# Scores of the first four head pairs from undivided float32 operands, 1e-9 as one more column of each score row, and a new set of due offsets, in a thresholded-attention and gated-mix kernel

## The chip, the cores and the metric

The kernel runs on one core of one Trainium2 chip. A time is device microseconds of that core for one execution. The profiled execution has its own time and a span, from its first instruction to its last; what lies around the span is launch and end.

## The reference, cut to what matters

There are 8 batches with 8 heads of 576 rows and 64 dimensions. The weights come in float64, everything else in float32.

```
scores = (q @ k.T) / sqrt(64)                     # per batch and head, 576 x 576
keep   = scores >= max(scores, -1) - tau
attn   = where(keep, exp(scores - max), 0)
attn   = attn / (sum(attn, -1) + 1e-9)
x      = attn @ v                                 # heads side by side: 576 x 512 per batch
gate   = sigmoid(sum_k conv_w[k] * x shifted by 4 - k rows)
out    = (gate * (x @ w_val)) @ w_out
```

## The kernel before, in words

**Pairs and tiles.** Two heads form a pair, and 4 pairs a batch: 32 pairs, each a `Job`. A pair's scores are cut into 9 tiles of 128 rows by 576 keys: for each of four blocks of 128 query rows one tile per head (h = 0 and h = 1), and one tile (h = None, the corner) that holds the first 64 query rows of both heads. There are 288 tiles, counted by k. A tile runs through TensorE (`multiply`, L732), the row maximum on VectorE (`largest`, L736), the threshold (`lowest`, L742, VectorE), the exponential on ScalarE (`weigh`, L746), and masking with the row sum on VectorE (`keep`, L753). Two tiles then form a group (a corner tile is one by itself): GpSimd adds 1e-9 to the sums (L770), VectorE takes reciprocals (`inv`, L772), GpSimd, ScalarE or VectorE divide (L779 to L783), TensorE transposes the result (L836), and ScalarE copies it out of PSUM (L847). When a pair's tiles are through, `attend` multiplies with v on TensorE (L876 and L883, later L914 and L922).

**Products in parts.** To keep float32 accuracy at TensorE's fast rate, q and k are split into a high and a low float32r part (L441 to L461: ScalarE makes the high part, GpSimd the low part), and the parts are copied by 16 DMAs per pair into operands in which the 128 contraction rows are 64 of one kind over 64 of another: `Q` holds the high and the low part of q one above the other, `KH` the high part of k twice, `KL` the low part twice. A head's tile is then four matmuls with 128 contraction rows (two halves of 288 keys, KH and KL each); a corner tile is six from `bdq`. The first pair has no time for that: `load_at_once` loads its operands already doubled and splits them itself (L579 to L615, corners L596 and L600), and its corner tile takes ten matmuls (L719).

**The mix.** After attention a pair's x goes through the five-tap convolution on VectorE (L993, four taps a pair; the first on GpSimd, L988). After the fourth pair of a batch come its 192 products with w_val and w_out (L1052). The weights are put together from their float64 words on VectorE, ScalarE and GpSimd (`from_f64`, L321 to L339, eight blocks).

**Order.** Every engine's order is fixed when the program is built. Each operation has a planned cost, a due time (its tile's number plus an offset from the table `EARLY` for tiles below 78 and from `AT` after them), and rooms (buffers) that it takes and gives; `carry_out` picks, again and again, the operation that can start first and is due first. An operation may have several engines to choose from. Queues run in that order; a late instruction holds back all that stands behind it on its engine. Where the plan sees TensorE idle for over 1 us before 115 us, it puts in products of the identity matrix that nothing reads (L181, `keep_busy`), and it starts the program with 11 of them; each is two instructions in the trace. Score rooms in PSUM: three until tile `THIRD_UNTIL`, then two, and the third one's banks become the accumulators of the products.

## Time and profile before

| what | value |
|---|---|
| median of 3 runs | 730.72 us (730.11 to 732.25) |
| the profiled execution | 731.91 us, of which span 730.1 us, so 1.8 us around it |
| TensorE busy | 710.7 us (97%) |
| VectorE busy | 659.6 us (90%) |
| ScalarE busy | 593.0 us (81%) |
| GpSimd busy | 470.7 us (64%) |

PE is TensorE, PEld its weight loads, DVE VectorE, ACT ScalarE, POOL GpSimd, SP the queue that issues most DMAs. A matmul's duration in the trace holds its way through the array, which overlaps with the next one; what a matmul really takes from the engine is the distance between two starts.

### The profile page before, as it was taken

To read this page: it belongs to the slowest core of one execution; us is meant where nothing else is said; L and a number is where in the kernel's file an instruction comes from. 1 tells how busy PE (TensorE), PEld (TensorE's weight loads), DVE (VectorE), ACT (ScalarE), POOL (GpSimd) and SP (SyncE) were. 2 spreads that over 40 slices of the span, in tenths; PEclk is the share of its full clock that TensorE was granted. 3 is DMA by queue.
4 is the path that set the end of the run, shared out by engine and by line. 5 is a ranking of instruction groups with operands and counts; after the bars stand their busy time and mean duration, and the time that the engine had idled before them with its cause. 6 is when DMAs were issued, how large, how long until landed. Compare 5 with 4: busy or idle time off the path is not lost.

```text
span 730.1 us, 16335 instructions
## 1 busy us (share of the span) xinstructions
PE 710.7 (97%) x5338; PEld 618.5 (85%) x5338; DVE 659.6 (90%) x1618; ACT 593.0 (81%) x1167; POOL 470.7 (64%) x690
## 2 busy tenths in 40 slices
PE   9889889999999999999999999999999999999998
PEld 9666667988888998888889888888988888898988
DVE  5989989999999988999999999999999999899842
ACT  5999988888878988877889887887978887898730
POOL 2787757887677747686566765667566865655231
PEclk9999989999999999999999999999999999999999
DMA  6777656527564665456665555556655446540001
GB/s 210 196 198 193 152 140 175 119 58 200 151 165 115 166 170 141 103 135 156 152 164 129 145 139 152 146 123 153 177 136 132 118 138 170 140 101 19 34 33 66
DMA packets 60884, 100.55 MB, mean 138 GB/s; under 512 B 18688, under 2 KB 20096, under 8 KB 60800
## 3 DMA queue, kind: packets, MB, share of 16 engines
q1 hardware_dynamic: 60512, 98.96, 52.7%
q8 instruction: 43, 0.70, 0.4%
q10 hardware_dynamic: 288, 0.56, 0.2%
q14 instruction: 41, 0.34, 0.1%
HBM read 35.18 MB, written 9.44 MB: 61 GB/s over the span
## 4 chain that ended last, share of the span: by engine, by line
PE 86%; DVE 7%; ACT 3%; issue 1%; DMA 1%; POOL 1%; SPq 0%; POOLq 0%; ACTq 0%; DVEq 0%
PE acc L1052 26%; PE s L732 20%; PE tp L836 17%; PE acc L922 9%; PE tp L922 6%; DVE pp L753 2%; PE tp L181 2%; PE acc L914 2%; DVE nm L736 2%; PE tp L914 2%; ACT e L746 1%; ACT T L847 1%; DMA KH<-kh 1%; PE tp L883 1%; DVE pre L993 1%
## 5 line engine op out<-in xcount | busy, mean ns | idle before, releaser
L736 DVE TENSOR_REDUCE nm<-s 128x1 f32<-128x576 f32 x276 | 204.8, 753 | 25.5 <-PE s L732 22.8
L746 ACT ACTIVATE e<-s,nm 128x576 f32<-128x576 f32 x276 | 204.4, 754 | 16.1 <-DVE nm L736 13.8
L753 DVE SCALAR_TENSOR_TENSOR pp<-s,th,e 128x576 f32<-128x576 f32 x244 | 196.9, 813 | 8.7 <-ACT e L746 4.4
L847 ACT COPY T<-tp 128x384 f32<-128x384 f32 x384 | 175.1, 493 | 17.8 <-PE tp L836 16.5
L836 PE MATMUL tp<-ident,pp 128*128 128x128 f32 x1152 | 176.8, 274 | 7.5 <-ACT T L847 5.1
L732 PE MATMUL s<-KH,Q 128*128 128x288 f32 x488 | 148.7, 321 | 4.2 <-DVE pp L753 3.5
L836 PEld LDWEIGHTS tp<-ident,pp 128*128 128x128 f32 x1152 | 137.1, 140 | 15.5 <-ACT T L847 7.9
L732 PE MATMUL s<-KL,Q 128*128 128x288 f32 x488 | 136.5, 296 | 0.0
L783 POOL TENSOR_SCALAR pp<-pp,sums 128x576 f32<-128x576 f32 x132 | 106.4, 811 | 27.7 <-DVE sums L772 12.0
L993 DVE SCALAR_TENSOR_TENSOR pre<-xT,cw,pre 128x576 f32<-128x576 f32 x128 | 119.8, 938 | 0.7
L732 PEld LDWEIGHTS s<-KH,Q 128*128 128x128 f32 x488 | 92.5, 190 | 18.7 <-issue 8.2
L779 ACT ACTIVATE pp<-pp,sums 128x576 f32<-128x576 f32 x102 | 79.4, 791 | 21.8 <-DVE sums L772 21.4
L770 POOL TENSOR_SCALAR sums<-sums 128x2 f32<-128x2 f32 (+1 forms) x160 | 45.0, 281 | 75.6 <-DVE pp L753 61.7
L732 PEld LDWEIGHTS s<-KL,Q 128*128 128x128 f32 x488 | 92.7, 190 | 0.0
L1052 PE MATMUL acc<-gh,woh 128*128 128x256 f32 (+1 forms) x256 | 78.8, 308 | 0.0
L1052 PE MATMUL acc<-xh,wvh 128*128 128x256 f32 (+1 forms) x256 | 78.5, 307 | 0.3 <-DVE pp L753 0.2
L1052 PE MATMUL acc<-gh,wol 128*128 128x256 f32 (+1 forms) x256 | 78.5, 307 | 0.0
L1052 PE MATMUL acc<-xh,wvl 128*128 128x256 f32 (+1 forms) x256 | 78.4, 306 | 0.0
L1052 PE MATMUL acc<-gl,woh 128*128 128x256 f32 (+1 forms) x256 | 78.1, 305 | 0.0
L1052 PE MATMUL acc<-xl,wvh 128*128 128x256 f32 (+1 forms) x256 | 77.8, 304 | 0.0
L447 POOL TENSOR_TENSOR kl<-k_r,kh 128x320 fp32r<-128x320 f32 x62 | 57.4, 933 | 25.4 <-ACT kh L441 15.9
L461 POOL TENSOR_TENSOR ql<-q_r,qh 128x320 fp32r<-128x320 f32 (+1 forms) x62 | 59.2, 971 | 21.8 <-ACT qh L455 20.6
(116 smaller groups left out, 1406.1 us busy)
## 6 DMA issues: line engine op xcount, KB each, us to landing
KH<-kh SPq DMA_DIRECT2D x124, 144.0 KB, 2.6
KL<-kl SPq DMA_DIRECT2D x124, 144.0 KB, 3.0
v<-vs SPq DMA_DIRECT2D x32, 320.0 KB, 3.0
k_r<-kT SPq DMA_DIRECT2D x31, 320.0 KB, 3.8
q_r<-qT SPq DMA_DIRECT2D x31, 288.0 KB, 3.1
outT<-o SPq DMA_DIRECT2D x28, 288.0 KB, 2.1
Q<-qh SPq DMA_DIRECT2D x62, 128.0 KB, 2.8
Q<-ql SPq DMA_DIRECT2D x62, 128.0 KB, 3.6
```

Source lines behind the costliest of these rows:

```text
L461: engine.tensor_sub(self.ql[:, x:y], self.q_r[:, x:y], self.qh[:, x:y].bitcast(F32))
L732: nc.tensor.matmul(s[:, a, :HS], w, m, start=i == 0, stop=i == len(terms) - 1)
L736: nc.vector.tensor_reduce(self.nm, self.s[:, :, :HS], axis=AX.XY, op=ALU.max, negate=True)
L746: nc.scalar.activation(self.e, self.s[:, :, :HS], AF.Exp, bias=self.nm)
L753: nc.vector.scalar_tensor_tensor(grp.p[:, i * S : (i + 1) * S].rearrange("p (a f) -> p a f", a=2), self.s[:, :, :HS], self.th, self.e, op0 ...
L779: nc.scalar.mul(v, v, ri(i))
L783: nc.gpsimd.tensor_scalar(v, v, ri(i), 0.0, op0=ALU.mult, op1=ALU.add)
L836: nc.tensor.transpose(tp[:, i * P : (i + 1) * P], self.p[:, k0 : k0 + P], ident)
L847: engine(T[:, c0 : c0 + n, self.off : self.off + P], tp[:, 0 : n * P].rearrange("p (c q) -> p c q", q=P),)
L922: nc.tensor.matmul(a[hs, : W[half.j]], t.v[:, c0 : c0 + D], half.T[:, h * NKC + c, 0 : W[half.j]], start=False, stop=c == NKC - 1, skip_gr ...
L993: nc.vector.scalar_tensor_tensor(cv, pair.xT[:, i + a : i + z], cw[:, g, i : i + 1], cv, op0=ALU.mult, op1=ALU.add)
L1052: nc.tensor.matmul(taken[name, e, j][:, :w], wt[:, c, c0 : c0 + P], moving(c, i)[:, hs], start=n == 0, stop=n == NM - 1,)
```

## The change

**Scores from whole float32.** For the first four pairs (`PLAIN = 4`) nothing is split and nothing copied. A head's tile is two float32 matmuls, one for each half of the keys, with 64 contraction rows (the head's 64 rows of the loaded k and q). A corner tile multiplies both heads' 64 x 64 blocks, four or five matmuls. q is still scaled once, now on GpSimd or VectorE. `load_at_once` loads one copy of the first pair's operands, with tau in a column of k that the product does not use.

**1e-9 as an element.** Each score room gets one more column that holds 3e38 and each exponential room one that holds 1e-9; `keep` runs over 577 elements, so that its sum contains 1e-9, and the addition on GpSimd (L770) is gone. The two halves of a score tile now lie side by side across the border of two PSUM banks.

**Choices and offsets.** `lowest` may run on GpSimd for every tile (`LOWEST` 0 to 300), `tap0` on ScalarE for tiles from 78 on. At the front 15 unread products instead of 11, and none are added for the gap before the first score. Room counts, due offsets and the planned pace of the products are new.

```
-PACE_M = 0.124
-THIRD_UNTIL = 38
-LOWEST = 0
+PACE_M = 0.147
+THIRD_UNTIL = 42
+LOWEST = 300
+PLAIN = 4
-HOLD = (1, 1)
+HOLD = (1, 4)
-    kr=1, qr=1, kh=2, kl=2, qh=1, ql=2, ...
+    kr=2, qr=2, kh=1, kl=2, qh=1, ql=1, ...
...            (tables AT and EARLY: nearly every offset is another one)
-FREE = ('out',)
+FREE = ('out', 'tap0')
-            if e == "PE" and 1.0 < gap and t < FILL_UNTIL and ...
+            if e == "PE" and 1.0 < gap and 0.0 < idle["PE"] and t < FILL_UNTIL and ...
+    def row(s):
+        return s.rearrange("p a f -> p (a f)")[:, 512 - HS : 512 - HS + S + 1]
+    for _, t in r_s.free:
+        nc.vector.memset(row(t)[:, S:], 3e38)
+    for _, t in r_e.free:
+        nc.vector.memset(t[:, S:], 1e-9)
...            (prepare, for the pairs 1 to 3, in place of the parts and their copies)
+            if self.plain:
+                self.whole = [got_k, op("POOL", ..., lambda: scale_q(nc.gpsimd), [got_q],
+                    other=[("DVEp", ..., lambda: scale_q(nc.vector))])]
+                self.give_raw = [(r_kr, lambda: self.k_r), (r_qr, lambda: self.q_r)]
+                return
...            (load_at_once)
+            for hs, queue in zip(HEADS, (nc.sync, nc.scalar)):
+                queue.dma_start(room[hs, 0:x], first[hs, 0:x])
+            nc.sync.dma_start(room[:, x : SK + n], first[:, x : SK + n])
+            nc.sync.dma_start(self.q_c, corner)
...            (multiply)
+                if t.plain:
+                    for i in range(2) if h is None else (h,):
+                        rows, ks = HEADS[i], SL * (h is None or h == 0) + a * HS
+                        to = s[rows if h is None else slice(0, P), hs]
+                        m = HS - SL * (h is None and i * a)
+                        for x, z, k0 in ((0, m, ks), (m, HS, 0)):
+                            if x < z:
+                                nc.tensor.matmul(
+                                    to[:, x:z], t.rows_q(rows, qc), t.k_r[rows, k0 : k0 + z - x],
+                                    start=True, stop=True, skip_group_check=True,
+                                )
...            (keep, turned)
-                grp.p[:, i * S : (i + 1) * S].rearrange("p (a f) -> p a f", a=2),
-                self.s[:, :, :HS], self.th, self.e,
+                grp.p[:, i * S : (i + 1) * S + 1], row(self.s), self.th, self.e,
-            add = op("POOL", ..., lambda: nc.gpsimd.tensor_scalar(
-                sums(), sums(), 1.0, 1e-9, op0=ALU.mult, op1=ALU.add), [self.kept])
-            inv = op("DVE", ..., lambda: nc.vector.reciprocal(ri(0, n), sums()), [add])
+            inv = op("DVE", ..., lambda: nc.vector.reciprocal(ri(0, n), sums()), [self.kept])
...
-    keep_busy(r_tp.free[0][1], 11)
+    keep_busy(r_tp.free[0][1], 15)
```

## Rows read from the trace of the kernel before

**Rows 1.** The span cut into stretches: busy time of each engine (and its instructions), then granted TensorE clock, DMA share and GB/s. 9.4 us is the start of tile 0's maximum, 86.6 of tile 36's, 698 the end of the last attention.

```profile
0.00:9.40 9.40, 8.04 (x46) 8.04 (x47) 2.48 (x8) 4.91 (x11) 1.29 (x10) 1.00 0.83 282
9.40:86.60 77.20, 68.03 (x486) 53.04 (x486) 73.11 (x194) 69.77 (x136) 56.56 (x80) 1.00 0.69 177
86.60:150.00 63.40, 59.33 (x401) 46.62 (x399) 60.02 (x142) 53.90 (x105) 46.09 (x60) 0.95 0.57 142
200.00:698.00 498.00, 497.94 (x3832) 439.63 (x3830) 466.25 (x1146) 415.03 (x817) 319.47 (x478) 1.00 0.52 133
```

**Rows 2.** TensorE's groups in the stretch from 8.57 to 88.5 us (first score to first product): out<-in, operand form, count | busy time, mean ns of one | idle before.

```profile
L836 PE MATMUL tp<-ident,pp 128*128 128x128 f32 x126 | 19.8, 281 | 5.9 <-ACT T L847 3.8 <-POOL pp L783 0.8 <-ACT xT L891 0.7
L732 PE MATMUL s<-KH,Q 128*128 128x288 f32 x42 | 13.5, 337 | 0.9 <-DVE th L742 0.6 <-DVE pp L753 0.3
L883 PE MATMUL tp<-T,v 128*64 128x320 f32 (+1 forms) x96 | 13.0, 412 | 0.0
...
L181 PE MATMUL tp<-ident 128*128 128x128 f32 x81 | 9.7, 275 | 0.0
...
L876 PE MATMUL tp<-T,v 128*128 128x320 f32 (+1 forms) x12 | 4.1, 420 | 0.5 <-ACT T L847 0.5
L836 PE MATMUL tp<-ident,pl 128*128 128x128 f32 x20 | 3.8, 286 | 0.9 <-ACT T L847 0.6 <-POOL pl L310 0.3
```

**Rows 3.** The chain that ended last, from 136.9 us on, a stretch in which TensorE runs without a gap: start, us, what. A piece's length is what it takes from the engine.

```profile
137.00 0.66 PE tp L836 x6
137.65 0.53 PE s L732 x4
...
138.74 1.41 PE acc L1052 x11
...
143.81 0.54 PE acc L914 x2
144.35 0.43 PE tp L914 x2
144.78 2.30 PE acc L922 x16
147.09 1.73 PE tp L922 x16
```

**Rows 4.** VectorE's costliest groups from 9.4 to 150 us, columns as in rows 2.

```profile
L736 DVE TENSOR_REDUCE nm<-s 128x1 f32<-128x576 f32 x47 | 35.1, 752 | 6.8 <-PE s L732 6.5
L753 DVE SCALAR_TENSOR_TENSOR pp<-s,th,e 128x576 f32<-128x576 f32 x39 | 31.5, 812 | 0.8 <-ACT T L847 0.4
L993 DVE SCALAR_TENSOR_TENSOR pre<-xT,cw,pre 128x576 f32<-128x576 f32 x16 | 15.7, 980 | 0.0
L742 DVE TENSOR_SCALAR th<-nm,less 128x1 f32<-128x1 f32 x58 | 10.5, 205 | 0.0
```

**Rows 5.** TensorE at the front, in order of time: start, us, what, count, idle before.

```profile
1.36 7.48 PE L181 MATMUL tp<-ident 128*128 128x128 f32 x40 [1.36 <-POOL ident masks.py:199]
8.60 0.38 PE L732 MATMUL s<-KH,Q 128*128 128x288 f32 x1
```

**Rows 6.** The unread products of the front, before and after 7.15 us: stretch, PE busy (instructions), PEld busy.

```profile
1.36:7.15 5.79, 5.79 (x27) 5.79 (x28) 1.00 0.95 302
7.15:8.57 1.42, 1.42 (x15) 1.42 (x14) 1.00 1.02 398
```

**Rows 7.** VectorE at the front and at one later place, in order of time.

```profile
4.06 0.15 DVE L579 TENSOR_SCALAR sc<-pp 128x1 f32<-128x1 f32 x1 [2.90 <-DMA pp<-first]
...
9.41 0.76 DVE L736 TENSOR_REDUCE nm<-s 128x1 f32<-128x576 f32 x1 [2.89 <-PE s L732]
10.21 0.49 DVE L600 SCALAR_TENSOR_TENSOR gh<-pl,sc,gh 64x64 fp32r<-64x64 f32 x2
10.61 1.43 DVE L615 SCALAR_TENSOR_TENSOR Q<-pp,sc,Q 64x128 fp32r<-64x128 f32 x3
...
16.45 0.33 DVE L742 TENSOR_SCALAR th<-nm,less 128x1 f32<-128x1 f32 x2
16.75 0.82 DVE L753 SCALAR_TENSOR_TENSOR pp<-s,th,e 128x576 f32<-128x576 f32 x1
```

**Rows 8.** GpSimd's groups from 9.4 to 150 us.

```profile
L447 POOL TENSOR_TENSOR kl<-k_r,kh 128x320 fp32r<-128x320 f32 x14 | 12.5, 896 | 13.0 <-ACT kh L441 12.6
L461 POOL TENSOR_TENSOR ql<-q_r,qh 128x320 fp32r<-128x320 f32 (+1 forms) x14 | 11.7, 842 | 1.1 <-ACT qh L455 0.7 <-DMA KL<-kl 0.3
L770 POOL TENSOR_SCALAR sums<-sums 128x2 f32<-128x2 f32 (+1 forms) x32 | 9.7, 303 | 8.0 <-DVE pp L753 5.4 <-DVE pl L753 0.9
L469 POOL TENSOR_SCALAR q_r<-q_r,sc 128x576 f32<-128x576 f32 x7 | 5.7, 819 | 0.5 <-DVE th L742 0.3
```

**Rows 9.** TensorE and its weight loads where it goes into, and comes back from, 64-column products: start, us, engine, what, count, idle before.

```profile
144.71 2.37 PE L922 MATMUL acc<-T,v 128*64 128x320 f32 x16
...
148.74 0.40 PE L732 MATMUL s<-KH,Q 128*128 128x288 f32 x1
148.98 0.29 PE L732 MATMUL s<-KL,Q 128*128 128x288 f32 x1
144.71 1.81 PEld L922 LDWEIGHTS acc<-T,v 128*64 128x64 f32 x16 [0.33 <-issue]
```

**Rows 10.** Maxima (L736) in VectorE's busy time in two stretches: one for each tile, the second with one that began before it.

```profile
9.40:86.60 77.20, 26.40 (x37) 1.00 0.69 177
200.00:687.60 487.60, 154.47 (x209) 1.00 0.53 135
```

**Rows 11.** What VectorE waited for in 150 to 700 us: us in total, times, longest.

```profile
DVE nm L736 <- PE s L732: 16.6, 43, 1.5
DVE pp L753 <- ACT e L746: 4.4, 13, 0.7
DVE sums L772 <- POOL sums L770: 1.8, 5, 0.8
```

More of the change, by code (lines that the diff above doesn't have):

```diff
@@ L56 @@
-    words_step=8.17, words_fetch=-14.64, split=119.57, words_sub=9.29, words2=-3.84, cw=-128.53,
-    corner=-82.08,
+    score=-1.7, largest=-155.73, lowest=172.23, weigh=-77.26, keep=135.29, add=34.01, inv=-108.3,
+    divide=115.08, turn=3.92, copy=-63.63, attend=-14.41, evac=-26.54, fetch=170.56, high_k=-42.79,
+    low_k=-89.88, scale_q=132.84, high_q=-68.15, low_q=-146.14, place=-61.21, copies=74.78,
+    copies_q=167.13, fetch_v=-24.97, prep=-4.29, early1=15.1, early2=13.7, early3=23.08,
@@ L58 @@
+    conv_high=44.47, tap0=-55.2, conv_low=103.23, tap=-107.06, tap_step=21, gate=-80.76,
+    products=16.37, val=-18.64, g_high=105.24, g_low=29.45, out=-6.45, send=49.79, words=4.52,
+    words_step=23.99, words_fetch=-6.81, split=17.4, words_sub=50.85, words2=-17.84, cw=-47.33,
+    corner=-65.66,
 )
@@ L557, in load_at_once @@
         def load_at_once(self):
-            b, g, n = self.pair.b, self.pair.g, self.n
-            rooms = [r_pp.take() for h in range(2)]
-            self.Q, self.KH, self.KL = r_Q.take(), r_KH.take(), r_KL.take()
-            cuts = [slice(0, P), slice(P, n)]
-            lo = HEADS[1]
-            k_r = [room[:, 0:S] for room in rooms]
-            q_r = [{0: room[:, S : S + P], 1: room[:, S + P + 1 : S + n + 1]} for room in rooms]
-            front = slice(0, S + P + 1)
-            back = slice(S + P + 1, S + n + 1)
@@ L568, in load_at_once @@
-            nc.sync.dma_start(rooms[0][:, front], first[0, :, front])
-            nc.scalar.dma_start(rooms[1][:, front], first[1, :, front])
-            for h, queue in enumerate((nc.sync, nc.scalar)):
-                queue.dma_start(rooms[h][:, back], first[h, :, back])
-            raw_c = r_pl.take()
-            nc.sync.dma_start(raw_c[:, 0:P], corner)
-            made_c = r_gh.take()
-            self.made_c = made_c
-            nc.vector.memset(made_c[:, 0 : 2 * P].bitcast(F32), 0.0)
@@ L658, in load_at_once @@
-            for h in range(2):
-                high = op("ACT", EARLY["corner"], act(SL) + 0.05, act(SL) + 0.2, high_c(h), got["c"])
-                self.corners.append(op("DVEp", EARLY["corner"], sub2(SL), sub2(SL) + 0.1, low_c(h), [high]))
-            op("SP", -30, 0.0, 0.0, lambda: None, self.corners, gives=[(r_pl, lambda: raw_c)])
-            op("SP", -30, 0.0, 0.0, lambda: None, used,
-               gives=[(r_pp, lambda room=room: room) for room in rooms])
+            n = self.n
+            room, room_c = r_pp.take(), r_pl.take()
@@ new lines, in load_at_once, with scaled @@
+            taus = [op("DVE", -30 + h, 0.16, 0.25, read_tau(h), got[str(h)]) for h in range(2)]
+            def scaled(what, q, rows, due, after):
+                m = q.shape[-1]
+                return op("DVEp", due, 0.07 + 0.00052 * m, 0.17 + 0.00052 * m, scale(q, rows, "DVE"), [*(taus[int(what) : int(what) + 1] if what in "01" else taus), *got[what], *after],
+                          other=[("POOL", pool1(m), pool1(m) + 0.1, scale(q, rows, "POOL"))] if what in "rc" else [])
+            self.first = [
+                scaled(str(h), self.q_r[hs, 0:P], hs, -29.5 + h, []) for h, hs in enumerate(HEADS)
+            ]
@@ L670, in __init__ @@
             both = h is None
-            if both and t.i == 0:
-                after = t.corners
+            if t.i == 0:
+                after = [*t.first, t.corner] if both else [t.first[h], *([t.rest] if qc else [])]
+            elif t.plain:
+                after = t.whole
             elif both:
                 after = [t.high_k, *t.low_k, *t.blocks]
-            elif t.i == 0:
-                after = [*t.first[h], *([t.rest[h]] if qc else [])]
             else:
@@ L997, in tap, with scaled, run, added @@
             return run
+        room = {}
+        def scaled(i):
+            def run():
+                room["tmp"] = r_tmp.take()
+                nc.scalar.mul(room["tmp"], pair.xT[:, i + a : i + z], cw[:, g, i : i + 1])
+            return run
+        def added():
+            cv = batch.pre[:, g, a:z]
+            nc.gpsimd.tensor_add(cv, cv, room["tmp"])
         def gate():
```

198 lines of the change are left out of this document (72 added, 126 removed).

## The prediction, made before the changed kernel was run

> **What bounds the kernel now.** I first cut the span into stretches [rows 1]. From 200 to 698 us TensorE is busy 497.94 of 498 us: there it is the bound, and no waiting of another engine matters. Before 150 us it isn't: from 9.4 to 86.6 us VectorE is busy 73.11 of 77.2 us, and from there to 150 us 60.02 of 63.4. There VectorE sets the pace, and the 36 tiles of the first batch take 77.2 us [rows 1, 10], 2.14 us a tile.
>
> What TensorE loses there is what can be won, and its busy time hides it, since the durations overlap. So I count instructions and price each by what it takes where TensorE runs without a gap [rows 3]: a transpose 0.11 us (0.66 for 6), a split score matmul 0.133 (0.53 for 4), a product 0.128 (1.41 for 11), a float32 product over 320 columns 0.54 (two instructions), over 256 columns 0.43, the 64-column part of one attention 2.30 + 1.73. From first score to first product, 79.9 us, the trace has 146 transposes (16.1 us), 166 score matmuls (22.1; the rows shown are the largest of their groups, the count is of all), three attentions (96 and 12 instructions, 15.0 us): 53.2 us of work [rows 2]. So 26.7 us are lost, 9.7 of them in unread products [rows 2]. The same count from 88.5 to 150 us gives 49.9 us of work in 61.5, so 11.6 lost, mostly in the first half. Together 38.3 us, and 7.5 us more ahead of 8.57, with next to nothing lost after 200 us.
>
> As the work that follows is fixed and TensorE does it without gaps, the end moves by as much as the point moves at which TensorE has caught up with VectorE's start, near 150 us. Two sums are needed: VectorE's load up to there, and whether TensorE's new work fits.
>
> **The front.** The 40 unread instructions end where the first score starts [rows 5], though its operands were ready before: VectorE had nothing to do for 2.89 us ahead of the first maximum [rows 7]. With 15 calls it will be 30 instructions and no more in the gap. Some 26 of 40 have started by 7.15 us, and the last 14 take 0.1 us each [rows 6], so the 30th ends near 7.5 us, and the first score starts there instead of at 8.60: 1.1 us gained. Its operands are there by then (tau was read at 4.06 us [rows 7] from a bigger load, and scaling 128 columns is less work than what is removed). A whole tile takes 0.44 us longer than a split one (below), so the first maximum comes 0.6 us earlier. The new memsets of one column lie in VectorE's 2.90 us of waiting for the first load [rows 7] and cost nothing.
>
> **VectorE's load up to 150 us.** Removed after the first maximum: splitting the first pair's queries and corners, 1.43 + 0.49 = 1.9 us [rows 7]. Added: scaling q, if it goes there. No row has a 576-column scaling on VectorE; on GpSimd it takes 0.82 us [rows 8], and the maximum over as many columns 0.75 on VectorE [rows 4]. Between nothing (all on GpSimd) and 4 x 0.75 = 3.0 I take 0.8. The threshold: 58 of them [rows 4]; two take 0.30 us from start to the next instruction (16.45 to 16.75 [rows 7]), so 0.15 each and 8.7 us in all. VectorE has little idle time in this stretch, GpSimd much (56.56 busy of 77.2 [rows 1]) and loses the splits of three pairs and the 1e-9 additions, so the order should give most of them to GpSimd; between 0 and 8.7 I take two thirds, 5.8. Idle time: VectorE's own is 7.5 us in 9.4 to 150 [rows 1], most of it behind scores [rows 4]; with fewer unread products in their way I take 2.0 of it as gained, between 0 and 5. The 577th element is 1/576 of 0.81 us, times 288 tiles 0.4 us, beside TensorE after 150 us and so nothing.
>
> Sum: 0.6 + 1.9 - 0.8 + 5.8 + 2.0 = 9.5 us.
>
> **Does TensorE's work fit?** No row has a product with 64 contraction rows in float32. The nearest is the one with 128: 0.54 us for 320 columns [rows 3], so 0.486 for 288, and a tile takes 0.97 instead of 4 x 0.133 = 0.53. Below that lies the split price (the tile costs nothing more), above it no reason. 32 such tiles make 14.1 us, the four corner tiles about 0.2 (0.97 if the two heads overlap as the 64-column products of attention do, 1.94 if they don't, so up to 4 more; I take the first, since 16 of those instructions take 2.30, that is 8 x 0.27 and a little [rows 3]). Then there is the change of shape. Going from whole-array products to 64-column ones, the weight load stood idle 0.33 us, and on the way back the first score is followed 0.24 us later by the next instead of 0.13 [rows 9]: 16 instructions took 2.30 where 8 x 0.27 = 2.16 would do, so 0.14 in and 0.11 out, 0.25 us a visit. Whether 64 contraction rows cost such a visit no row shows. Bounds 0 and 36 x 0.25 = 9.0; I take half, 4.5, since about every second tile follows another.
>
> The Trainium skill (TensorEngine Tiling (Array Packing), Key Properties) says that a change of tiling mode, not only of the tile, drains TensorE, and it counts 64 x 128 as a mode of its own. The 0.25 us a visit agree with it for 64 columns; for 64 rows nothing here shows it. By that rule the term is 9.0, without it 0.
>
> So 14.1 + 0.2 + 4.5 = 18.8 us of new work meet 38.3 us of loss; 19.5 are left, and after shortening by 9.5 10.0 of some 130 us, 8%. That fits, but no more than just: a gain of 15 would need TensorE at 97% while three score rooms wait on the softmax chain.
>
> **What I cost at nothing.** The removed L770 (45 us of GpSimd by the page) and its step ahead of the reciprocal: covered by TensorE's bound after 200 us; VectorE waited for it 1.8 us in all [rows 11], and that is the bound. The copies and splits of three pairs: they end on ScalarE, GpSimd and the DMAs, and the raw loads come earlier. `THIRD_UNTIL` 42 lets the products begin four tiles later: four tiles on which TensorE has 14.5 / 9 = 1.6 us of attention for 2.1 us (14.5 is 38 score matmuls, 41 transposes and one attention of 5.0), so up to 2 us, within the 10.0. The other rooms, `tap0` and the offsets after 150 us: no loss stands there to be won, and a worse order could only lose (the fourth rival).
>
> From the profiled execution: span 730.1 - 9.5 = 720.6, with 1.8 around it 722.4. That execution is 1.2 us above the median, so 721.2 on the median.
>
> **Rivals.**
> First, the forecast: VectorE's relief carries through. 716 to 726 us. For it speaks that VectorE is busy 95% from 9.4 to 150 us. Chance 0.52.
>
> Second, more than that: all 58 thresholds go (2.9 more), the idle time by 5 instead of 2 (3.0 more) and no scaling on VectorE (0.8 more) give 714.5. Or neighbouring tiles of the two heads, which lie in different contraction rows, overlap: with half of the 16 neighbours of four pairs that is 8 x 0.97 = 7.8 us and no visit (4.5) off TensorE, which makes room for this; no row shows two halves of the contraction rows together. On this the Trainium skill (TensorE: Matmul & The Clock Gate, Part 3) says that products in different row groups run concurrently. About 713. Chance 0.18.
>
> Third, TensorE becomes the bound in the first batch: each whole tile pays its visit (9.0), corners don't overlap (4). Then 53.2 + 14.1 + 0.2 + 13.0 = 80.5 us of work, at 94% 85.6, end at 7.5 + 85.6 = 93.1 instead of 88.5, 4.6 later. VectorE uses the time for weights and taps, so that of the 11.6 us lost behind it half or more comes back, and 1 to 2 lost by 200 us: 726 to 732. For it speaks the 8% above. Chance 0.18.
>
> Fourth, slower: the threshold on GpSimd is late. It must come before the exponential ends, some 0.75 us after the maximum, or `keep` and all behind it on VectorE wait. GpSimd's instructions last 0.8 to 0.9 us [rows 8] and can't be broken off. From 200 to 698 us VectorE has 31.7 us of slack [rows 1] on 209 tiles [rows 10], 0.15 a tile, and gains 0.15 by the move: beyond a mean wait of 0.30 us a tile VectorE becomes the bound, and each 0.1 more costs 21 us. At 0.37 that is 15 us, less the 9.5 won at the front: 736. Against it speaks that the planned order gives GpSimd a threshold only where it sees it free. Chance 0.12.
>
> **How the numbers follow.** The likeliest case gives 721.2 us. The range is 712 to 731: it takes in the forecast, the second rival and nearly all of the third (0.85 together), and leaves out the fourth. About 0.3%, 2.2 us, is what a measurement of this kernel can tell from no change (728.5 to 732.9). Faster: the forecast, the second rival and half of the third, 0.52 + 0.18 + 0.09 = 0.79. Within 0.3%: most of what is left of the third, and a little of the fourth, 0.10. Slower: 0.11.
>
> **What would show it.** Right: the first score near 7.5 us; L742 mostly on GpSimd; tile 36's maximum 4 to 8 us ahead of 86.6 us; two float32 instructions of one half 0.24 us apart; TensorE without gaps from some 140 us on; no wait of VectorE for a GpSimd threshold above 0.3 us a tile. Wrong: the first product (or tile 42) later than now, gaps of TensorE around each whole tile, or new gaps after 200 us behind `keep`.

## The result, and the profile after

The changed kernel takes 736.78 us in the median of 5 runs (735.22 to 739.6); the kernel before, timed beside it, 730.72 us (729.39 to 732.25). The ratio is 1.0081, with a 95% interval of 1.0052 to 1.0111: slower by 6 us, where 721.2 us was predicted. The profiled execution took 736.78 us, its span 735.0 us. The same stretches as in [rows 1], with 150 to 200 us added:

```profile
0.00:9.40 9.40, 7.41 (x42) 6.54 (x42) 3.26 (x17) 2.23 (x3) 1.28 (x10) 1.00 0.75 218
9.40:86.60 77.20, 74.28 (x401) 45.69 (x402) 68.65 (x170) 61.65 (x116) 46.96 (x58) 0.98 0.33 101
86.60:150.00 63.40, 60.70 (x432) 48.54 (x432) 58.92 (x145) 57.09 (x112) 47.91 (x60) 1.00 0.64 157
150.00:200.00 50.00, 47.70 (x346) 41.24 (x345) 45.36 (x103) 42.08 (x85) 26.07 (x36) 0.97 0.53 145
200.00:698.00 498.00, 495.47 (x3816) 438.79 (x3815) 451.47 (x1047) 421.88 (x831) 298.13 (x453) 1.00 0.52 132
```

Two things differ from before. From 9.4 to 86.6 us TensorE is busy 74.28 us (68.03 before) and VectorE only 68.65 (73.11): the bound of the first batch has changed hands. And after 200 us TensorE, which had no gap, now loses 2.5 of 498 us.

Where in the kernel the time goes is read best from the starts of single maxima:

| start of the maximum of tile | before | after | difference |
|---|---|---|---|
| 0 | 9.4 us | 7.8 us | -1.6 |
| 36 (end of the first batch) | 86.6 | 91.9 | +5.3 |
| 60 | 153.9 | 153.9 | 0.0 |
| 108 | 266.3 | 268.9 | +2.6 |
| end of the last maximum | 687.5 | 692.3 | +4.8 |

So the change gains 1.6 us at the front, loses 6.9 by the end of the first batch, wins 5.3 back up to tile 60, and from tile 60 on, where the prediction had costed it at nothing, it loses 4.8 us. The loss at tile 36 is partly one of order: ahead of it VectorE now does 8 taps of the convolution and 27 instructions on weight words, where it did 4 and 24.

The chain that ended last shows what the new tiles cost (start, us, what; x4 is one head's tile):

```profile
6.63 1.18 PE s L686 x8
11.69 2.19 PE s L686 x8
...
16.67 1.16 PE third L686 x4
18.31 1.18 PE s L686 x4
...
35.49 1.17 PE s L686 x4
37.13 1.16 PE third L686 x4
39.32 1.88 PE tp L848 x16
41.20 1.17 PE s L686 x4
```

From 6 to 60 us score tiles make 45% of this chain; in the kernel before they made 10% of it, beside VectorE, ScalarE, GpSimd and transfers. Most take 1.16 to 1.18 us, not 0.97. The first line is an exception and the second another, and both come up again below: tiles 0 and 1 took 1.18 us together, and the corner 2.19.

What VectorE does before tile 36 is seen in two lines for the thresholds (busy time of VectorE, then of GpSimd, from 7.8 to 91.9 us and on to tile 60), and in the costliest wait:

```profile
7.80:91.90 84.10, 4.72 (x26) 3.12 (x9) 0.98 0.38 112
91.90:153.90 62.00, 4.34 (x23) 0.52 (x2) 1.00 0.62 157
```
```profile
L703 DVE TENSOR_REDUCE nm<-s 128x1 f32<-128x576 f32 x24 | 18.0, 754 | 7.0 <-PE s L686 6.6
```

Only 11 of the first 60 thresholds went to GpSimd, and VectorE stood 6.6 us waiting for whole tiles. From the first maximum to tile 60 (before, then after; columns as in [rows 1]) VectorE's work fell by 3.6 us, and its idle time rose from 8.2 to 13.4 us:

```profile
9.40:153.90 144.50, 131.05 (x911) 102.96 (x911) 136.30 (x342) 127.53 (x248) 106.56 (x143) 0.98 0.63 159
7.80:153.90 146.10, 139.84 (x866) 98.33 (x865) 132.67 (x327) 122.90 (x235) 98.48 (x122) 0.99 0.48 131
```

After tile 60 there are two gaps. From 150 to 230 us, before (first fence) and after (second), in steps of 5 us and one of 30; columns as in [rows 1]:

```profile
155.00:160.00 5.00, 3.91 (x30) 3.64 (x30) 4.87 (x13) 4.33 (x8) 4.83 (x7) 1.00 0.39 89
160.00:165.00 5.00, 5.00 (x41) 4.87 (x41) 4.53 (x13) 4.96 (x12) 4.66 (x8) 1.00 0.36 83
...
200.00:230.00 30.00, 30.00 (x236) 27.49 (x234) 28.79 (x74) 25.73 (x51) 23.76 (x36) 1.00 0.67 156
```
```profile
155.00:160.00 5.00, 3.42 (x19) 2.94 (x19) 4.87 (x10) 5.00 (x10) 4.49 (x5) 0.85 0.21 47
160.00:165.00 5.00, 5.00 (x35) 4.99 (x35) 4.37 (x12) 4.10 (x9) 2.45 (x3) 0.81 0.53 122
...
200.00:230.00 30.00, 28.47 (x212) 24.73 (x211) 25.82 (x64) 27.46 (x53) 20.42 (x31) 1.00 0.50 122
```

The instruction counts tell more than the busy time. In 155 to 165 us TensorE started 54 instructions, 71 before. It waited 1.7 us in one piece, and then ran at a granted clock of 0.85 and 0.81. The chain there goes through ScalarE, step by step: exponentials, copies of transposes, the split of a gate (L1083) and, among them, the rounding of a weight block (L396):

```profile
151.06 1.41 ACT e L713 x2
...
153.28 0.58 ACT gh L1083
153.85 0.52 ACT woh L396
...
154.73 0.74 ACT e L713
155.47 0.37 ACT T L812
155.84 0.68 ACT pp L744
156.52 0.04 issue
156.57 0.66 PE tp L801 x4
```

The weight words were the thread that I followed: before tile 36 VectorE of the changed kernel did 27 instructions on them (12.7 us), and 13 more up to tile 60.

### The profile page after: what moved, and what is told of

It reads as the page before. It is cut to its first block, busy times and chain, and to the rows that moved or that the text cites. A ratio compares the mean times of both kernels' runs of the same rounds, so it can differ in the third digit from the quotient of the medians.

```text
span 735.0 us, 16013 instructions
## 1 busy us (share of the span) xinstructions
PE 719.5 (98%) x5282; PEld 612.2 (83%) x5282; DVE 642.4 (87%) x1506; ACT 591.5 (80%) x1157; POOL 429.1 (58%) x626
## 4 chain that ended last, share of the span: by engine, by line
PE 82%; DVE 5%; ACT 5%; POOL 3%; issue 2%; DMA 2%; SPq 1%; POOLq 0%; ACTq 0%; DVEq 0%
PE acc L1035 24%; PE s L699 17%; PE tp L801 16%; PE acc L887 8%; PE tp L887 6%; PE s L686 3%; DVE pp L721 2%; ACT e L713 2%; PE acc L879 2%; PE tp L848 2%; DVE nm L703 1%; PE tp L879 1%; PE third L686 1%; DMA q_r<-qT 1%; PE tp L184 1%
## 5 line engine op out<-in xcount | busy, mean ns | idle before, releaser
L721 DVE SCALAR_TENSOR_TENSOR pp<-s,th,e 128x577 f32<-128x577 f32 x242 | 195.8, 815 | 19.6 <-ACT e L713 14.3
L812 ACT COPY T<-tp 128x384 f32<-128x384 f32 x384 | 175.9, 492 | 19.5 <-PE tp L801 18.1
L801 PE MATMUL tp<-ident,pp 128*128 128x128 f32 x1152 | 180.9, 275 | 5.8 <-ACT T L812 2.4
L699 PE MATMUL s<-KH,Q 128*128 128x288 f32 x444 | 135.0, 322 | 1.5 <-DVE pp L721 1.4
L699 PE MATMUL s<-KL,Q 128*128 128x288 f32 x444 | 123.2, 294 | 0.0
L958 DVE SCALAR_TENSOR_TENSOR pre<-xT,cw,pre 128x576 f32<-128x576 f32 x128 | 109.3, 854 | 1.4
L699 PEld LDWEIGHTS s<-KH,Q 128*128 128x128 f32 x444 | 83.6, 188 | 14.1 <-issue 5.4
L699 PEld LDWEIGHTS s<-KL,Q 128*128 128x128 f32 x444 | 83.9, 189 | 0.0
L953 POOL TENSOR_SCALAR pre<-xT,cw 128x576 f32<-128x576 f32 x32 | 25.8, 806 | 90.8 <-ACT xT L897 84.6
L887 PE MATMUL acc<-T,v 128*64 128x320 f32 x432 | 64.1, 439 | 0.0
L469 POOL TENSOR_TENSOR kl<-k_r,kh 128x320 fp32r<-128x320 f32 x56 | 49.1, 879 | 16.4 <-ACT kh L463 16.2
```

What stands on the lines that cost most here:

```text
L469: engine.tensor_sub(self.kl[:, x:y], self.k_r[:, x:y], self.kh[:, x:y].bitcast(F32))
L699: nc.tensor.matmul(s[:, hs], w, m, start=i == 0, stop=i == len(terms) - 1)
L721: nc.vector.scalar_tensor_tensor(grp.p[:, i * S : (i + 1) * S + 1], row(self.s), self.th, self.e, op0=ALU.is_ge, op1=ALU.mult, accum_out=g ...
L801: nc.tensor.transpose(tp[:, i * P : (i + 1) * P], self.p[:, k0 : k0 + P], ident)
L812: engine(T[:, c0 : c0 + n, self.off : self.off + P], tp[:, 0 : n * P].rearrange("p (c q) -> p c q", q=P),)
L887: nc.tensor.matmul(a[hs, : W[half.j]], t.v[:, c0 : c0 + D], half.T[:, h * NKC + c, 0 : W[half.j]], start=False, stop=c == NKC - 1, skip_gr ...
```

## The experiments

The theories at the start: the whole tile's own price (a visit to the 64-row shape; the products themselves), the extra column, GpSimd as a place for thresholds, and the order of the work. All kernels were timed beside the kernel before, whose medians were 730.4 to 731.1 us; ratios are against it. The kernels whose names begin with a_ are made from the changed kernel, those with b_ from the kernel before; most differ from it in one thing.

**a_rows.** A head's tile multiplies all 128 contraction rows, so it gives the sum of both heads' scores; instructions, columns and waits are otherwise the same.

```
+                        if h is not None:
+                            rows = slice(0, P)
```

> The changed kernel with the head tiles of the first four pairs multiplied over all 128 contraction rows, so that a tile is the sum of both heads' scores; nothing else differs, and TensorE never goes into the 64-row shape for them. Theory V (the 0.2 us by which a whole tile exceeds 0.97 us is the change of shape): a whole tile falls from 1.17 to about 0.98 us, 32 of them give 6 us back in the first batch, tile 36's maximum comes near 86 us instead of 91.9, and the span falls by 4 to 6 us. Rival K (64 contraction rows are slow in themselves, or the whole tile isn't on the path): tile and span stay, or the tile shortens and the span stays within 2 us.

Measured: 730.99 us (728.87 to 732.04, 10 runs), ratio 1.0003 (0.9991 to 1.0015), 5.8 us less than the changed kernel. One tile between its neighbours, here and then in the changed kernel (start, us, engine, what, count):

```profile
30.63 0.55 PE L803 MATMUL tp<-ident,pp 128*128 128x128 f32 x3
31.01 1.14 PE L688 MATMUL s<-k_r,q_r 128*128 128x288 f32 x4
31.98 0.82 PE L803 MATMUL tp<-ident,pp 128*128 128x128 f32 x6
```
```profile
31.80 0.55 PE L801 MATMUL tp<-ident,pp 128*128 128x128 f32 x3
32.28 1.23 PE L686 MATMUL s<-k_r,q_r 64*128 64x288 f32 x4
33.45 0.87 PE L801 MATMUL tp<-ident,pp 128*128 128x128 f32 x6
```

From start to start the tile is 0.97 us with 128 rows and 1.17 with 64, 0.20 us more. Its neighbours are held up as well: the tile begins 0.48 instead of 0.38 us after the three transposes ahead of it, and the six transposes behind it take 0.87 instead of 0.82 us. The whole visit is thus some 0.35 us. Ahead of tile 36 the changed kernel makes 29 visits and this one 4, for the corners, so 25 fall away, some 8.7 us of TensorE; against that stands that two heads' tiles can't overlap here (see below). Tile 36 came at 86.1 us, 5.8 earlier, tile 60 at 148.8, 5.1 earlier, and the whole kernel gained 5.8. Two other things changed with the visit and are not told apart from it: the tile now takes what the plan holds it for, and the granted clock no longer fell at the front, which a_warm below puts at 1 us or less.

**a_upper.** The whole scores from the upper 16 bits of each number, read as bfloat16: the price of a float32 product goes, the precision too.

```
+   upper = lambda x: x.bitcast(mybir.dt.bfloat16).rearrange("p (n t) -> p n t", t=2)[:, :, 1]
...
-   to[:, x:z], t.rows_q(rows, qc), t.k_r[rows, k0 : k0 + z - x],
+   to[:, x:z], upper(t.rows_q(rows, qc)), upper(t.k_r[rows, k0 : k0 + z - x]),
```

> The changed kernel with the whole-operand scores multiplied from the upper 16 bits of every element of k and q as bfloat16 (one instruction of one pass instead of two of two), which leaves most of the precision out; the order of all engines is the same. A tile should take about 0.44 us instead of 1.17 on TensorE, 24 us less over the first batch. Theory P (TensorE's new work in the first batch is what moved the end): VectorE becomes the bound there, tile 36's maximum comes at 80 to 84 us, and the span falls by 7 to 11 us. Rival O (the loss lies in the new order, after the first batch): tile 36 may come earlier, but the span stays within 2 us of 735.

Measured: 733.98 us (731.26 to 736.1), ratio 1.0045 (1.0031 to 1.0059). Tile 36 came at 85.3 us, 6.6 earlier, but the time fell by only 2.8, which fits neither theory.

```profile
9.40:86.60 77.20, 62.44 (x352) 34.80 (x351) 73.09 (x186) 64.87 (x127) 52.17 (x64) 0.89 0.39 117
```

With TensorE far below its limit VectorE is busy 73.09 of 77.2 us again, just as before the change. So what VectorE was relieved of doesn't bring tile 36 forward in this order: the four more taps and three more instructions on weight words stand in its place. At tile 60 (149.0 us) 4.9 us are gained, not 9.5. TensorE, with less to do, was granted 0.89 of its clock, so this run doesn't show VectorE's limit alone.

**b_eps_fixed.** The extra column and the contiguous rows alone, in the old order (the step of L770 stays in the plan, empty):

```
-   lambda: nc.gpsimd.tensor_scalar(sums(), sums(), 1.0, 1e-9, op0=ALU.mult, op1=ALU.add)
+   lambda: None
...
+   nc.vector.memset(row(t)[:, S:], 3e38)      # and 1e-9 in the exponentials' rooms
```

> The kernel before with the 1e-9 as one more element of each row and the two halves of a score tile side by side, nothing else; the planned order is kept (the addition stays in the plan and issues nothing). Forecast: nothing, within 1.5 us of before, since VectorE waited 1.8 us in all for the addition and TensorE is the bound after 200 us. Rival: rows across two banks cost VectorE or ScalarE time, the maximum, exponential or masking last longer than 753, 754 and 813 ns, and the span grows by more than 2 us.

Measured: 733.79 us (730.49 to 735.69, 10 runs), ratio 1.0039 (1.002 to 1.0057). The maximum takes 753 ns (753 before) and `keep` 815 (813), so there's no price for the bank border in these instructions. The time is 3.3 us above the kernel before, where 1.5 at most was expected. Three of the ten runs lay at 730.5 to 731.0, all with a mean granted clock of 1.00, the others above 733, all but one of them with 0.995 to 0.998. What the 3 us are stays open, and with it how much of them is in the changed kernel, where this part wasn't undone. It doesn't gain anything.

**b_low_fixed.** All thresholds on GpSimd in the kernel before, at the places that the old order gives them on VectorE:

```
-   lambda: self.lowest(nc.vector)
+   lambda: self.lowest(nc.gpsimd)
```

> The kernel before with every threshold on GpSimd instead of VectorE, at the place in time at which the plan had it; all other work in the same order. Forecast's step: VectorE is relieved of 0.15 us a tile up to 150 us and the span falls by 3 to 8 us. Rival (the fourth): GpSimd's long instructions make thresholds late, VectorE waits for them by more than 0.3 us a tile on average, and the span grows by 5 us or more.

Measured: 747.99 us (747.66 to 748.3), ratio 1.0237 (1.0222 to 1.0252).

```profile
DVE pp L753 <- POOL th L742: 38.2, 79, 1.7
```

That is my fourth rival's mechanism: VectorE waits 38.2 us for late thresholds. Its price was too kind: the wait is 0.13 us a tile on the mean of 288, where the rival needed more than 0.30, and the time rose by 17 us all the same.

**a_low_dve.** The reverse in the changed kernel: its 106 thresholds on GpSimd are issued on VectorE, in the same order.

```
-   other=[("POOL", 0.26, 0.36, lambda: self.lowest(nc.gpsimd))]
+   other=[("POOL", 0.26, 0.36, lambda: self.lowest(nc.vector))]
```

> The changed kernel with every threshold on VectorE: the 106 that the plan gives to GpSimd are issued on VectorE at the same place in time, all else is the same. If the choice of engine is worth what the prediction said (0.15 us of VectorE each where VectorE is the bound), only the few before 150 us count, about 11 of them, 1 to 2 us, and the rest lie beside TensorE: 0 to 3 us slower than the changed kernel. Rival (a threshold on GpSimd costs VectorE a wait, as in the kernel before with all of them there): faster than the changed kernel by 2 us or more.

Measured: 739.93 us (739.37 to 740.78), ratio 1.0124 (1.01 to 1.0148), 3.1 us more. Where the plan picks the place, the move is worth 3 us, a little more than the 0 to 3 expected. It isn't what made the change slower.

**a_cost.** One number of the plan: what a whole tile costs TensorE.

```
-   cost = 0.98
+   cost = 1.17
```

> The changed kernel with one number of its plan mended: a whole tile is planned at the 1.17 us that the trace shows, not at 0.98. Offsets as they are, so the order changes from there on. Theory W (the order of the changed kernel is wrong because the plan thinks TensorE free 0.2 us too early after each whole tile): the waits of 150 to 230 us shrink and the span falls by 2 us or more. Rival (the offsets themselves are unfit, whatever the price): the span stays within 2 us of the changed kernel's 735 or grows.

Measured: 730.53 us (730.29 to 733.21, 10 runs), ratio 0.9998 (0.9982 to 1.0015), 6.2 us less than the changed kernel with the same operations. Tile 36 came later still, at 93.6 us, but tile 60 at 151.8, and what follows ran without the two gaps:

```profile
155.00:160.00 5.00, 4.72 (x38) 4.42 (x37) 4.41 (x12) 4.63 (x10) 5.00 (x7) 1.00 0.37 82
160.00:165.00 5.00, 5.00 (x39) 4.63 (x37) 4.30 (x12) 4.96 (x12) 2.50 (x6) 1.00 0.94 212
...
200.00:230.00 30.00, 29.88 (x229) 25.96 (x229) 28.42 (x66) 27.34 (x53) 20.94 (x32) 1.00 0.56 131
```

Knowing that TensorE was taken for 1.17 us, the plan gave VectorE 38 instructions on weight words (21.2 us) before tile 36 instead of 27 (12.7), and 20 taps instead of 16 by tile 60. VectorE's idle time from the first maximum to tile 60 is 5.6 us here and 13.4 in the changed kernel: work that fits into its waiting was done there. That this is what closes the gaps behind tile 60 isn't shown. By tile 60 all 40 instructions of the first weights are done in the kernel before (24 ahead of tile 36 and 16 behind), in the changed kernel (27 and 13) and here (38 and 2) alike.

**a_cost079 and a_cost136.** Controls with the same number at 0.79 and 1.36.

> The changed kernel with one number altered: a whole tile is planned at 0.79 us of TensorE (0.98 in the changed kernel, 1.17 in a_cost, 1.17 measured). Control for a_cost. If what a_cost gained (6 us) came from planning a tile at what it takes, the error is now twice as large (0.38 us a tile, 12 us over 32 tiles) and the time is above the changed kernel's 736.8: 738 to 744, with fewer weight-word instructions on VectorE ahead of tile 36 than the 27 of the changed kernel. If any other order would have done as well as a_cost's, this one is as likely to gain: 728 to 737.

> The changed kernel with one number altered: a whole tile is planned at 1.36 us of TensorE, 0.19 more than was measured. Second control for a_cost (730.5). If the right price matters, this side errs too, but with the harmless sign: VectorE gets more filling work than it has gaps for, tile 36 comes 1 to 4 us later than a_cost's 93.6, and TensorE waits for tiles it could have had: 731 to 736. If it is only that a dearer whole tile puts more filling work early, it goes on gaining: 726 to 730. If orders scatter by a few us whatever the price: anywhere from 728 to 740.

Measured: 740.18 us (739.65 to 741.66), ratio 1.0119, and 734.15 us (731.12 to 738.23, 10 runs), ratio 1.0039 (1.0016 to 1.0062). So 0.79, 0.98, 1.17 and 1.36 give 740.2, 736.8, 730.5 and 734.2 us. The least is at 1.17, the tile from start to start. With the whole visit a tile takes some 1.32 us, though, which is nearer to 1.36, and each price gives one order only. The four runs show that this one number moves the same operations by some 10 us. That the right price gives the best order is likely, but not shown. With 0.79 TensorE is busy 6.99 of 10 us from 150 to 160. With 0.79 VectorE's instructions on weight words were 27 before tile 36, not fewer than the changed kernel's 27 as I had expected.

**a_oldoffsets.** The changed kernel with the offsets, pace, `THIRD_UNTIL` and key and query rooms of the kernel before.

> The changed kernel with the due offsets, pace, THIRD_UNTIL and the six rooms of keys and queries (kr, qr, kh, kl, qh, ql) of the kernel before, all other parts of the change kept; its planned price of a whole tile stays 0.98. If the new offsets by themselves were what made the changed kernel slower, this is faster than its 736.8: 726 to 733. If the offsets belong to the work that they were made for, the old ones suit the new work worse: 740 to 757, with tile 60 later than 154 us or waits at the first products.

Measured: 762.44 us (761.62 to 771.78), ratio 1.0449 (1.0396 to 1.0502), worse than expected. Tile 36 came at 133.3 us in the profiled execution, the one of 771.78 us. The new offsets aren't bad in themselves, they are far better for this work than the old ones. But they were found with a tile at 0.98 us, which isn't what it costs.

**a_offsets.** The same work once more, with the tile priced at 1.17, an unread product at 0.235 instead of 0.115 us, and all due offsets, the pace and `THIRD_UNTIL` (40) found anew under these prices.

> The changed kernel with 1.17 us for a whole tile and 0.235 us for an unread product in its plan, and with all due offsets (and the products' pace, and 40 for 42 in THIRD_UNTIL) searched anew for a short plan; the work of every engine is the same. Theory S (the new work of the first batch and the loss taken out of it cancel, and the 5 us by which the changed kernel is slower lie in its order between 150 and 230 us): tile 60's maximum stays near 154 us, TensorE's new gaps behind it go, and the time falls by 4 to 7 us, to 730 to 733. Rival B (the first batch's new work on TensorE is the whole price): no order can give it back and the time stays within 2 us of 736.8.

Measured: 725.72 us (725.56 to 725.9, 4 runs), ratio 0.9929 (0.9907 to 0.9952): 11 us below the changed kernel, 5 below the kernel before. Tile 60 came at 147.5 us, 6.4 earlier than in either; I had expected it to stay and the time to end at 730 to 733.

```profile
86.60:150.00 63.40, 61.98 (x455) 51.48 (x456) 60.86 (x144) 61.16 (x120) 48.37 (x60) 1.00 0.61 155
150.00:200.00 50.00, 49.98 (x388) 44.79 (x387) 45.29 (x107) 42.94 (x91) 28.10 (x41) 1.00 0.56 147
200.00:698.00 498.00, 497.05 (x3822) 438.38 (x3821) 457.27 (x1086) 417.02 (x825) 269.99 (x394) 1.00 0.51 131
```

**n4.** No visits for pairs 1 to 3: each head's queries in a 128-row tile whose other rows are zero, keys of both heads one above the other, corners from a block-diagonal tile, keys scaled instead of queries, nine unread calls in front, `THIRD_UNTIL` 46, fewer rooms for q and k, and the order found anew with 0.98 for these tiles and 1.17 for those of the first pair.

```
+   if t.plain and t.i:
+       w = t.cz if h is None else t.qz[h][:, qc * P : (qc + 1) * P]
...
+       nc.tensor.matmul(s[:, hs], w, t.k_r[:, ks : ks + HS], start=True, stop=True)
...
-   cost = 0.98
+   cost = 0.98 if t.i else 1.17
```

> The changed kernel with the whole scores of pairs 1 to 3 made without a change of shape: each head's queries stand in a 128-row tile whose other 64 rows are zero, the keys of both heads lie one above the other and are scaled in place of the queries, and the corners come from a block-diagonal tile. The order is made anew for this work, as in a_offsets, from prices that were measured (1.17 us for a tile of pair 0, 0.98 for the others). If the visit of the 64-row shape (0.19 us a tile by a_rows) and the order's wrong prices are what cost the changed kernel its gain, the two remedies add up: the 24 head tiles give 24 x 0.19 = 4.6 us of TensorE beyond a_offsets (725.7), less a little for the zeros and the extra transfers, so 721 to 723 us, with two instructions of a padded tile 0.49 us long each as those of a_rows, and tile 60 some 3 us ahead of a_offsets' 147.5. If a_offsets was only a lucky order, another order made in the same way lands anywhere between 725 and 735. If the padded queries arrive late (three more transfers in the first 30 us), tiles 9 to 36 are late and the time is above 726.

Measured: 717.65 us in the median, ratio 0.9844 (0.9793 to 0.9896), better than expected; four executions took 716.5 to 718.1 us at a mean granted clock of 0.998 to 1.000, two 726.6 and 726.8 at 0.986. One of these two was profiled:

```profile
9.00:12.00 3.00, 2.41 (x6) 1.35 (x8) 2.24 (x7) 2.10 (x3) 1.20 (x3) 0.61 0.82 257
12.00:15.00 3.00, 3.00 (x16) 2.10 (x14) 2.35 (x5) 0.93 (x2) 0.41 (x2) 0.50 1.02 354
15.00:18.00 3.00, 3.00 (x8) 1.62 (x8) 1.24 (x5) 1.97 (x4) 2.11 (x4) 0.50 0.70 280
...
27.00:30.00 3.00, 3.00 (x9) 2.14 (x9) 1.49 (x3) 1.23 (x3) 0.27 (x1) 0.50 0.01 3
```

TensorE stood idle 1.53 us ahead of tile 3, which waits for a score room, and then ran at half its clock, 1.2 instead of 2.4 GHz, until 30 us.

**n4_warm, a_warm.** Six unread calls between the scores of tiles 2 and 3, in n4 and in the changed kernel; **a_front20**: 20 calls in front of the changed kernel instead of 15.

```
+            if self.k == 3:
+                keep_busy(r_tp.free[0][1], 6)
```

> n4 with one edit: six unread products (12 instructions of about 0.1 us) between the scores of tiles 2 and 3, where TensorE stood idle for 1.53 us in n4's profile; all else in the same order. In that profile the granted clock was 0.61 from 9 to 12 us, 0.50 from 12 to 30 and 1.00 after, although TensorE was busy 3.00 of 3.00 us from 12 on; the time was 726.56, and four other executions at a mean clock of 0.998 to 1.000 took 716.5 to 718.1. If the idle time is what lets the clock fall, all executions are now at 716.5 to 718.5 with a mean clock of 0.998 or more, and 1.00 in every stretch of 3 us from 9 to 30. If the fall comes from something else (the float32 products of 64 rows themselves, or the chip), the group near 726 stays, with 0.50 at 12 to 30 us in its profile.

> The changed kernel with the same edit: six unread products between the scores of tiles 2 and 3. It fills the 1.53 us from 8.8 to 10.3 us in which TensorE stood idle before its granted clock fell to 0.50 at 12 us. If the clock matters, it stays at 1.00 from 12 to 18 us, the corner's 10 instructions (2.19 us at the low clock) take about half, tiles 4 to 9 come 1 to 2 us earlier, and the time is 733 to 735.5 (the changed kernel's own executions at a clock of 0.998 took 735.2 and 735.4, those at 0.993 to 0.995 736.8 to 739.6). If the clock at 12 us costs nothing, because VectorE sets the pace there, it is 736 to 738. In neither case does it come down to 730.7: the order after 150 us is unchanged.

> The changed kernel with 20 unread products in front instead of 15, so 40 instructions as the kernel before had ahead of its first score (22 in front and 18 in the first gap): this part of the change undone. The prediction put it at 0.6 us of gain: then the first score comes 1 us later, near 7.6 us, and the time is 0.5 to 1 us above the changed kernel's, 737 to 738, with the clock falling as it did, since the idle time between tiles 2 and 3 is still there. If the products in front are what holds the clock up from 12 us on, it is 733 to 736 with 1.00 there.

Measured, n4_warm: 717.15 us (716.83 to 717.67, 5 runs), mean clock 1.000 in each, ratio 0.9811 (0.9787 to 0.9836). The second group is gone, and no stretch of 3 us up to 45 us lies below 1.00. This is the fastest version, 13.3 us below the kernel before.

```profile
9.40:86.60 77.20, 74.28 (x423) 50.47 (x425) 75.79 (x193) 69.84 (x136) 57.38 (x73) 1.00 0.49 143
...
200.00:698.00 498.00, 497.97 (x3841) 442.29 (x3838) 454.46 (x1031) 424.93 (x833) 292.93 (x427) 1.00 0.51 129
```

Measured, a_warm: 735.83 us (733.92 to 737.74, 7 runs), ratio 1.006 (1.0039 to 1.0082). The clock stayed at 1.00 at the front, and the corner's ten instructions took 1.20 us instead of 2.19. In this execution the first score came 1.1 us later than in the profile of the changed kernel; tile 9 was 0.4 us earlier all the same, so 1.6 us were won there, and at tile 36 still 0.4. At the end the 1 us between the medians is inside their ranges: for the changed kernel the fall of the clock at the front is not what decides.

Measured, a_front20: 739.79 us (737.64 to 740.61), ratio 1.0115 (1.0083 to 1.0147), 3 us more than the changed kernel. The first score came at 8.74 us, 2.2 later, tile 36 2.2 later. The clock fell as before. The first score is 1.0 us later than in a_warm's profile, which has the changed kernel's 15 calls. So fewer products in front are worth 1 to 3 us, not 0.6.

## Why the prediction was wrong

**What was right.** A whole tile costs 0.97 us of TensorE apart from the visit. The two heads of a corner overlap (1.12 to 1.19 us with the visit, where the high bound was 4 us more for the four). The front gave more than the 0.6 us: in the profiled execution the first score started at 6.56 us, the first maximum 1.6 us earlier. Part of that is luck, since behind the same 15 calls the first score started only at 7.23 us in a_low_dve and at 7.70 in a_warm. L770 and the extra column cost nothing on their own engines. The reason given against the fourth rival held: where the plan picked the places, VectorE waited 0.6 us in all for a threshold on GpSimd.

**VectorE's load, the sum of 9.5.** It came out at nothing. In its own terms, up to tile 60: the front 1.6 for 0.6, the splits 1.9 as costed, no scaling on VectorE behind the first maximum for 0.8, the thresholds 1.7 for 5.8 (11 of them at 0.15 us, where two thirds of 58 were to go), and for the idle time a loss of 5.2 (8.2 us, then 13.4) where 2.0 had been taken as gained. That makes 0.0 for 9.5, and tile 60 starts at 153.9 us in both kernels. The two steps that failed are the thresholds, for which GpSimd's room had been taken as a mean over the stretch, and the idle time, which hangs on TensorE.

**Does TensorE's work fit.** This step decides over the idle time. The change of shape was a term between 0 and 9.0, taken at 4.5; 29 visits of some 0.35 us are 10, above the bound. But the size isn't the main failure. That is the sentence that 18.8 us of new work "fits" because 38.3 are lost. Counted in the same way, TensorE's lost time up to tile 60 (unread products, waits, visits, the front) fell from about 48 to 33 us, that is by 15, and the 32 tiles take 14.1 more. Gain and price cancel. Of the 33, 6.6 are the front and 10 the visits, so some 16 stayed lost and didn't serve to shorten anything; the prediction had left 19.5 and let the shortening take 9.5 of them. A share of 92% over 130 us was worked out as a mean; in the first batch alone it was 74.28 of 77.2 us, and with three score rooms each late tile makes VectorE wait and each late `keep` TensorE. The mechanism is that of my third rival, TensorE as the bound of the first batch, which had a chance of 0.18. Its figures weren't right: the corners do overlap, and the first product was to come at 93.1 us. It came at 109.1, where it had been at 88.5, one of the signs that I had named; n4_warm, the fastest version, has it at 107.2, so that sign says little. That tile 36 is late by 5.3 us, close to the rival's 4.6, is luck.

**What I cost at nothing.** "The other rooms, `tap0` and the offsets after 150 us: no loss stands there to be won, and a worse order could only lose (the fourth rival)." The second half was right, and without a price. From tile 60 to the end of the last maximum the changed kernel loses 4.8 us. In 155 to 165 and 200 to 230 us TensorE stands idle 3.1 us (1.1 before), and at 0.85 and 0.81 of the clock it loses another 1.7. The experiments keep the two parts apart:

| | tile 36 | tile 60 | from tile 60 to the end of the last maximum |
|---|---|---|---|
| before | 86.6 us | 153.9 us | 533.6 us |
| after | 91.9 | 153.9 | 538.4 |
| a_rows | 86.1 | 148.8 | 537.6 |
| a_upper | 85.3 | 149.0 | 539.6 |
| a_cost | 93.6 | 151.8 | 534.7 |
| a_cost136 | 95.8 | 156.6 | 536.7 |
| a_cost079 | 91.4 | 156.3 | 541.8 |
| a_offsets | 90.0 | 147.5 | 534.0 |
| n4_warm | 81.7 | 139.8 | 534.7 |

Cheaper tiles in the changed kernel's order (a_rows, a_upper) gain 5 us ahead of tile 60 and leave the loss behind it. Another order (a_cost, a_offsets) takes most of that loss back with the dear tiles. So the loss behind tile 60 lies in the order and not in what the tiles take when they run. One altered price in the plan takes the 6 us back in all (730.5), 2.1 of them ahead of tile 60, and a new order with all offsets found again 5 us more. My first reading, that the plan with a tile at 0.98 us sees no waiting of VectorE and leaves the weight words for later, doesn't explain the gaps: n4_warm does 26 instructions on weight words ahead of tile 36, fewer than the changed kernel's 27, and has no gap behind tile 60. Which operation makes them stays open. `cost = 0.98` stands in the kernel, beside the 0.97 that I had worked out without the visit and a visit that I had put at up to 0.25 us. A plan that agrees with an estimate isn't evidence for it.

**The visit and the overlap.** The visit of some 0.35 us, from the rows of a_rows, agrees with the Trainium skill (TensorEngine Tiling (Array Packing), Key Properties), by which a change of tiling mode drains TensorE; I had given the rule half weight. The other place of the Trainium skill that I had cited, TensorE: Matmul & The Clock Gate, Part 3, says that products in different row groups run together. The trace shows it where the two heads' tiles stand side by side, at the front: eight instructions of tiles 0 and 1 begin at 6.56 us and the next tile at 7.63, 1.07 us for two tiles. That half of my second rival is real, but almost everywhere else a transpose, an attention or a wait lies between the two heads. Where they do follow each other directly, at 26.66 us, they still took 2.10 us; what held the second one back isn't shown. An order that pairs them throughout wasn't tried.

**What stays open.** Whether the extra column costs 0 or 3 us (b_eps_fixed), which operation makes the gaps behind tile 60, and how much of n4's 8 us below a_offsets is the visits (24 of some 0.35 us make 8.4) and how much its own order. Whether a new order alone would also make the kernel before faster wasn't tried either.

## What to carry to other kernels

A hand-planned order is part of the kernel's cost: when an operation changes, measure one, write its price into the plan and make the order anew before judging the change; here 0.19 us in one number was worth 6 us, and the same operations ran anywhere from 725.7 to 762.4 us. Lost time on an engine isn't room for new work until one knows why it is lost: check the fit in the stretch where the engine would be fullest, not over the mean. And a gap of 1.5 us at the front deserves a look at the granted clock behind it.

## What the runs showed of the hardware

A float32 product with 64 contraction rows costs some 0.35 us more for each group of them that stands between products with 128, by the starts in the traces of the changed kernel and a_rows (0.20 us in the group and 0.15 in its neighbours); the same product over 128 rows, half of them zero, costs nothing more (0.97 us a tile in n4_warm).

After 1.53 us of idle TensorE ahead of tile 3 the granted clock fell to half in every profile that has this gap (the changed kernel, a_cost, a_cost136, a_offsets, a_oldoffsets, a_low_dve, a_front20, n4), for 3 to 7 us, and in n4 for some 20 us, in which TensorE was busy: 9 us of n4's time. In the changed kernel:

```profile
10.29 1.24 PE L686 MATMUL s<-pp 64*128 64x288 f32 x4 [1.53 <-DVE pp L721]
12.00:15.00 3.00, 3.00 (x15) 2.11 (x12) 2.44 (x6) 1.82 (x4) 2.10 (x3) 0.50 0.39 160
```

It stayed at 1.00 in the profiles where the gap was filled (a_warm, n4_warm, and a_cost079, whose plan filled it) or shorter (a_rows, 0.78 us). Such a gap doesn't always do it. In the kernel before, TensorE stood idle as long ahead of 37.44 us, and the clock stayed at 1.00:

```profile
37.44 0.93 PE L836 MATMUL tp<-ident,pp 128*128 128x128 f32 x6 [1.53 <-ACT T L847]
36.00:39.00 3.00, 1.56 (x12) 1.49 (x13) 2.92 (x11) 3.00 (x7) 2.23 (x5) 1.00 0.51 118
39.00:42.00 3.00, 2.95 (x24) 1.95 (x24) 3.00 (x8) 3.00 (x6) 2.85 (x3) 1.00 0.86 208
```

And of n4's six executions three show a mean clock of 1.000. What makes the difference isn't shown. The gap at 155 us was followed by the same fall in the changed kernel (0.85 and 0.81 over 10 us), so there a wait on the critical path was paid a second time.
